# Fused thresholded attention and hard-swish layer: another order of work in the last slots and the tail

## The chip, the cores and the metric

One core of a Trainium2 chip runs the whole kernel. The metric is the time of one execution on the device, in microseconds (us); for the kernel before it is 521.78 us, the median of three runs (521.37 to 523.26). Profiles are of one execution; their span (521.3 us for the kernel before) is counted from its first to its last instruction. TensorE multiplies, VectorE and ScalarE work on the results, GpSimd does one step of the softmax, and SyncE's queue issues most transfers.

## The reference

Attention over 8 batches, 8 heads, 576 tokens and 64 dimensions, in which scores that lie more than `tau` below the row's maximum are rejected, and then a layer with two products and a hard-swish between them over all 4608 tokens:

```
scores = (q @ k.T) / sqrt(64)
scores = where(scores >= max(scores) - tau, scores, -1e9)
attn   = exp(scores - max(scores));  attn = attn / (sum(attn) + 1e-9)
x      = (attn @ v), heads side by side           # 4608 x 512
h      = x @ w_in                                 # 4608 x 2048
g      = h * clip(h + 3, 0, 6) / 6
out    = g @ w_out                                # 4608 x 512, f32
```

## The kernel before

**Slots.** The 64 heads are taken in 16 groups of four (a "quad", two pairs of heads). A batch has two quads. The 576 query rows are four blocks of 128 and a remainder of 64. Each quad has nine slots: four blocks for each pair, and one slot for the remainder rows of both pairs. So there are 144 slots, numbered 0 to 143, and one loop that runs over them (L518). In slot n the scores of slots further on are multiplied (`scores`, L287, one or two slots ahead), VectorE takes the maximum of slot n + 1 while it copies the scores out of PSUM (`sm_max`, L302), ScalarE masks and exponentiates (L309, L314), VectorE takes the reciprocal of the sums (L317), GpSimd multiplies by it (`sm_norm`, L322), and a DMA transpose issued by SyncE (L330) turns the rows of attention around for the product with the values (`av`, L346 and L349). The transposed tiles are called `pT` for the blocks of 128 rows and `pR` for the remainder slot.

**The layer.** It follows behind the attention, item by item. An *item* (`mm1`) is a first product of 512 columns in one PSUM bank: eight products 256 wide for the main tokens (L381), or four products 512 wide for the *odd tokens*, the 64 remainder rows of two batches together (L376). ScalarE (L389) or VectorE (L391) forms the clamp `r` from it, and VectorE gates it (`mm1_gate`, L404) into `g`. The clamp has two tiles. For odd tokens the gate writes a separate tile `go`, two items to a tile, and a DMA transpose (L406) brings that into `g`; there is one `go` tile only, so the third odd gate can't begin before the first transpose has read it. A *token tile* (`mm2_part`, four parts of four products) is 128 tokens of the second product: 16 products 512 wide (L415), an eviction with the factor 1/6 (L421 on ScalarE, L423 on VectorE) and a store (L436).

**Queues.** `todo1` holds items, `todo2` holds parts of token tiles; a tile's parts enter `todo2` when the last item that it needs has been multiplied. Each slot takes one item, each even slot two parts as well. `moe_of(b)` lists the items of batch b: the columns 0 to 255 first, in eight items, then the odd tokens (batches with odd numbers only, four items), then the columns 256 to 511 in eight items. For odd batches the last two odd items are put behind two of the others (L447).

**Banks.** PSUM has eight banks (`ps`). In the loop, items and tile parts use the banks 6 and 7 (`HB`, `OB`), scores 0, 1, 3, 4 and halves of 2 and 5, and the attention product 2 and 5. An even slot's item and the following odd slot's share bank 6 if the even slot had tile parts.

**The tail.** All of this is written out by hand: each engine does its work in the order in which the program lists it. After the loop there is (L649 to L663): the third quarter of the last quad's attention product, the two items left in `todo1` (batch 6, clamp on VectorE), the reciprocal and the multiplication for slot 143, the eight *head* items of batch 7, the last attention product of the blocks and that of the remainder rows (`av_rest`), all tile parts that wait in `todo2`, the twelve *tail* items of batch 7 (four odd items, eight main ones) and the last three token tiles. Here the items go round the banks 0, 1, 3 and 4 (`rest1`, beginning with bank 1), and the tiles alternate between the banks 7 and 6 (`rest2`).

Of the kernel before, what the change touches and what calls it, by code (L numbers as in the profile page):

```python
# [20 lines left out]
def kernel(  # L21
# [11 lines left out]
    B, H, S, D = q.shape  # L33
# [8 lines left out]
    N1 = 22  # L42
    N2 = 28
    HB, OB = 6, 7
# [138 lines left out]
    def warm_up(count):  # L183
        for _ in range(count):
            nc.tensor.transpose(ps[:, HB, 0:P], identf[:], identf[:])
# [23 lines left out]
    now = -1  # L209
    turn = 0  # L210

    def bank():
        nonlocal turn
        turn += 1
        return ps[:, (2, 5)[turn % 2], :]
# [96 lines left out]
    def sm_exp(sl, i):  # L312
        s = sl.s[:, i, :]
        nc.scalar.activation(out=s, in_=s, func=Act.Exp, accum_out=sl.rsum[:, i:i + 1])  # L314

    def sm_recip(sl):
        nc.vector.reciprocal(out=sl.rinv[:], in_=sl.rsum[:])  # L317
# [23 lines left out]
    def av(pb, pair, pT, cols):  # L341
        b, hp = divmod(pair, NPAIR)
        vm, vr = vsb[b]
        for c in range(4):
            for a in range(2):
                nc.tensor.matmul(pb[a * 64:(a + 1) * 64, :], vm[:, 2 * hp + a, c * D:(c + 1) * D],  # L346
                                 pT[:, 5 * a + c, cols], start=(c == 0), stop=False)
        for a in range(2):
            nc.tensor.matmul(pb[a * 64:(a + 1) * 64, :], vr[:, a, hp, :], pT[:, 4, cols], start=False, stop=True)  # L349

    def av_main(pair, c0=0, w=512):
        b, hp = divmod(pair, NPAIR)
        if hp == c0 == 0:
            xT[b] = x_pool.tile([P, KI, 512], BF16, tag="xT", name="xT")
        pb = bank()[:, 0:w]
        av(pb, pair, pts[pair], slice(c0, c0 + w))
        return lambda: nc.vector.tensor_copy(out=xT[b][:, hp, c0:c0 + w], in_=pb)  # L357
# [14 lines left out]
    def mm1(item, hb=HB):  # L372
        b, ni, c0 = item
        if c0 is None:
            for ki in range(KI):
                nc.tensor.matmul(ps[:, hb, :], xR[b // 2][:, ki, :], w_in_sb[:, ki, ni * P:ni * P + 512],  # L376
                                 start=(ki == 0), stop=(ki == KI - 1))
        else:
            for n in range(2):
                for ki in range(KI):  # L380
                    nc.tensor.matmul(ps[:, hb, n * 256:(n + 1) * 256], w_in_sb[:, ki, (ni + n) * P:(ni + n + 1) * P],  # L381
                                     xT[b][:, ki, c0:c0 + 256], start=(ki == 0), stop=(ki == KI - 1))
        return ps[:, hb, :]
# [27 lines left out]
    def mm2_part(bb, mt, part, ob=OB):  # L411
        if part == 0:
            o_ps[0] = ps[:, ob, :]
        for ni in range(part * 4, part * 4 + 4):
            nc.tensor.matmul(o_ps[0], gbuf[:, ni, mt * P:(mt + 1) * P], w_out_sb[:, ni, :],  # L415
                             start=(ni == 0), stop=(ni == NI - 1))
# [14 lines left out]
    todo2 = []  # L431
# [8 lines left out]
    def moe_of(b):  # L440
        items = []
        for c0, mts in (((0, (5, 6)), (None, (4,)), (256, (7, 8))) if b % 2 else ((0, (0, 1)), (256, (2, 3)))):
            for ni in range(0, NI, 4 if c0 is None else 2):
                items.append(((b, ni, c0), ()))
            items[-1] = (items[-1][0], [(b // 2, mt, part) for mt in mts for part in range(4)])
        if b % 2:
            items[10:14] = items[12:14] + items[10:12]  # L447
        return items[0:8], items[8:]

    alloc_qk(0)  # L450
# [18 lines left out]
    queue = []  # L469
# [34 lines left out]
    def multiply(n):  # L504
# [6 lines left out]
                todo1.extend(moe_of(of // 2)[0])  # L511
        return copies

    prev = None
    last_keys = []
    part = 0
    waiting = []
    for n, sl in enumerate(queue):  # L518
        quad, slot = sl.quad, sl.slot
        b, g = divmod(quad, 2)  # L520
        now = n
        if slot in (0, 4):
            pts[2 * quad + slot // 4] = pt_pool.tile([P, 9, 512], BF16, tag="pT", name="pT")
        if slot == 8:
            ptr[quad] = ptr_pool.tile([P, 9, P], BF16, tag="pR", name="pR")
        for ahead in {0: (1, 2), 9: (3,), 16: (4,)}.get(n, (quad + 2,) if quad > 2 and slot == (2 if quad == 3 else 0) else ()):
            if ahead < NQUAD:
                load_quad(ahead)
        if slot == 0 and g == 1 and b + 1 < B:
            load_v(b + 1)  # L530
        for copy in last_keys:
            copy()
        last_keys = []
        if 0 < n <= N1:
            for i in range(2):
                sm_exp(prev, i)
        if n + 1 < len(queue):
            sm_max(queue[n + 1])
        even = n >= N1 and n % 2 == 0
        if n > N1:  # L540
            sm_recip(prev)
        for copy in waiting:
            copy()
        waiting = []

        if todo1:
            item, then = todo1.pop(0)
            h = mm1(item, OB if n > N1 and n % 2 and not pieces else HB)
            todo2.extend(then)
        else:  # L550
            item = None
        if n >= N1:
            for copy in multiply(n):
                copy()
        if item:
            mm1_gate(item, h, mm1_relu(h, on_act=even))
        copies = pe_transpose(queue[n - 2]) if n > 1 and queue[n - 2].on_chip else None
        if prev is not None and n < N1:
            sm_recip(prev)
        if copies:  # L560
            copies()
        pieces = 2 if n % 2 == 0 and todo2 else 0
        for _ in range(pieces):
            bb, mt, part = todo2.pop(0)
            mm2_part(bb, mt, part)
        if n <= N1:
            for i in range(2):
                sm_mask(sl, i)
        if n == N1:
            sm_recip(prev)  # L570
        if n >= N1:
            for i in range(2):
                sm_exp(sl, i)
            if n + 1 < len(queue):
                for i in range(2):
                    sm_mask(queue[n + 1], i)
        if n < N1:
            for copy in multiply(n):
                copy()
        if part == 3:  # L580
            waiting.append(lambda tile=(bb, mt): late.extend(mm2_out(*tile, on_act=False)))
            part = 0
        evict = []
        for job, of in turns.get(n, ()):
            if job == "k":
                (last_keys if even else evict).append(transpose_k(of))
            elif job == "q":
                if of // 2 not in qkT:
                    alloc_qk(of // 2)
                (waiting if even else evict).append(transpose_q(of))  # L590
            else:
                (last_keys if even else evict).append(transpose_rest(of, of_k=of > 0))
        for out_of_psum in evict:
            if out_of_psum:
                out_of_psum()
        if n == 0:
            warm_up(8)
        if n <= N1:
            scores(n + 2)
        elif n % 2:  # L600
            for m in (n + 3, n + 2):
                if m < len(queue):
                    scores(m)
        if n < 8:
            warm_up(6)
        if n > 0:
            sm_norm(prev)
        flush()
        if n == 0:
            start(loads, 2)  # L610
        elif n not in (4, 12, 15, 18, 21) and not 23 < n < 30 and (n < 37 or n % 2 == 0):
            start(loads, 1)
        if n < 4 or 15 < n < 20 or n > 33:
            start(vcasts, 1 if n < N1 or n % 2 else 0)
        else:
            start(casts, 2 if n in (5, 8, 11, 14) or 21 < n < 28 else 1)
        prev = sl
# [13 lines left out]
    def rest1(item, then, on_act=True):  # L631
        h = mm1(item, hb=(0, 1, 3, 4)[count[0] % 4])
        count[0] += 1
        mm1_gate(item, h, mm1_relu(h, on_act))
        todo2.extend(then)

    def rest2():
        while todo2:
            bb, mt, part = todo2.pop(0)
            mm2_part(bb, mt, part, ob=OB - count[1] % 2)  # L640
            if part == 3:
                flush()
                if (bb, mt) == (B // 2 - 1, 8):
                    last_out()
                else:
                    late.extend(mm2_out(bb, mt, on_act=(count[1] % 2 == 0)))
                count[1] += 1
# [4 lines left out]
    sm_recip(prev)  # L652
    sm_norm(prev)
    head, tail = moe_of(B - 1)
    for item in head:
        rest1(*item)
    av_main(2 * last + 1, 256, 256)()
    av_rest(last)()
    rest2()
# [38 lines left out]
```

## Time and profile before

| what | value |
|---|---|
| time, median of three runs | 521.78 us (521.37 to 523.26) |
| span of the profiled execution | 521.3 us |
| TensorE busy | 503.0 us, 96% of the span |
| VectorE, ScalarE busy | 442.5 us (85%), 451.9 us (87%) |
| GpSimd busy | 299.3 us (57%) |
| slot 142's item begins on TensorE | 464.49 us |
| the tail's first items begin (L381 x80) | 469.27 us |
| `av_rest` begins | 479.77 us |
| tile parts between head and tail begin (L415 x70) | 480.44 us |
| tail items begin (L376) | 495.76 us |
| last three token tiles begin, TensorE ends | 507.16 us, 517.5 us |

In a timeline, a line has the start, the length, the engine, the line of the kernel, the operation with its output and input tiles and shapes, and a count of instructions that were merged; in brackets stand the idle time of the engine ahead of it and what ended it. PE is TensorE's stream of products, PEld its loading of weights, DVE is VectorE, ACT ScalarE, POOL GpSimd and SPq the queue of SyncE. The ends of products are modelled, and a few per cent of their records can be missing (70 of 72 products have one in a group above).

### The profile page before, as it was taken

What the parts mean: (1) busy time and instruction counts of PE and PEld (TensorE: products, weight loads), DVE (VectorE), ACT (ScalarE), POOL (GpSimd) and SP (SyncE); (2) the same over time, 40 slices, a digit from 0 to 9 for tenths busy, and PEclk for the clock granted to TensorE, in tenths of its full rate; (3) what the DMA queues carried; (4) which work ended last, traced back from release to release, by engine and by line L of the source; (5) the groups of instructions that cost most, each with busy time, mean ns of one, the idle gap of its engine ahead of it and who ended that gap; (6) DMA issues with size and microseconds to landing.
All of it is one profiled execution on the core that took longest, in us unless ns stands there. A gap on an engine that the chain in (4) does not pass through costs nothing.

```text
span 521.3 us, 12068 instructions
## 1 busy us (share of the span) xinstructions
PE 503.0 (96%) x4089; PEld 321.4 (62%) x4145; DVE 442.5 (85%) x1124; ACT 451.9 (87%) x980; POOL 299.3 (57%) x538
## 2 busy tenths in 40 slices
PE   8999999999999999999999999999999999999997
PEld 6765556666665666666665666666655666667463
DVE  3788888998999989999999999999999999877151
ACT  3999979999999989999999999999999999995060
POOL 1788869756676656657566656657566755551000
PEclk9999999999999999999999999999999999999999
DMA  5899999999999999999989999999999996574222
GB/s 131 123 174 157 155 150 139 152 177 177 160 168 178 160 181 168 173 165 187 178 148 162 181 179 160 176 159 177 165 160 171 183 162 113 112 117 65 82 61 60
DMA packets 314094, 78.77 MB, mean 151 GB/s; under 512 B 296624, under 2 KB 309168, under 8 KB 314032
## 3 DMA queue, kind: packets, MB, share of 16 engines
q1 hardware_dynamic: 294464, 67.90, 77.6%
q0 software_dynamic: 18368, 9.71, 15.7%
q8 instruction: 32, 0.52, 0.4%
q10 hardware_dynamic: 1200, 0.39, 0.3%
q14 instruction: 30, 0.25, 0.2%
HBM read 36.70 MB, written 9.44 MB: 89 GB/s over the span
## 4 chain that ended last, share of the span: by engine, by line
PE 69%; ACT 5%; DMA 4%; DVE 3%; issue 2%; POOL 2%; SPq 1%; POOLq 0%; DVEq 0%
PE ps L287 22%; PE ps L415 21%; PE ps L381 18%; PE ps L346 6%; PE ps L376 2%; ACT s L309 2%; DMA pT<-pn 2%; POOL pn L322 2%; ACT s L314 2%; DVE s L302 1%; ACT r L389 1%; PE ps L349 1%; DMA pR<-pn 1%; DVE g L404 1%; DMA nq<-in_q_dram 1%
## 5 line engine op out<-in xcount | busy, mean ns | idle before, releaser
L322 POOL TENSOR_SCALAR pn<-s,rinv 128x576 bf16<-128x576 f32 x288 | 210.6, 743 | 19.1 <-issue 4.4
L302 DVE TENSOR_SCALAR_CACHE_REDUCE s<-ps 128x576 f32<-128x576 f32 x288 | 205.1, 749 | 17.6 <-PE ps L287 9.0
L309 ACT ACTIVATE s<-s,bias 128x576 f32<-128x576 f32 x288 | 205.8, 763 | 6.0 <-POOL bias L305 5.7
L314 ACT ACTIVATE s<-s 128x576 f32<-128x576 f32 x288 | 192.5, 671 | 0.3
L287 PE MATMUL ps<-kT,qT 64*128 64x384 f32 (+7 forms) x1280 | 174.0, 419 | 4.7 <-DVE s L302 3.8
L287 PEld LDWEIGHTS ps<-kT,qT 64*128 64x128 f32 (+1 forms) x1280 | 103.6, 175 | 59.3 <-issue 15.8
L381 PE MATMUL ps<-xT,w_in_sb 128*128 128x256 bf16 x1024 | 130.8, 273 | 1.2 <-DVE g L404 0.7
L415 PE MATMUL ps<-w_out_sb,g 128*128 128x512 bf16 x524 | 123.4, 379 | 2.8 <-issue 0.2
L381 PEld LDWEIGHTS <-w_in_sb 128*128 128x128 bf16 x1024 | 95.5, 98 | 41.0 <-issue 22.0
L305 POOL TENSOR_SCALAR bias<-m 128x2 f32<-128x2 f32 x144 | 26.9, 187 | 155.5 <-DVE rinv L317 135.8
L404 DVE SCALAR_TENSOR_TENSOR g<-r,ps 128x512 bf16<-128x512 f32 x128 | 87.6, 687 | 9.5 <-ACT r L389 5.5
L415 PEld LDWEIGHTS <-g 128*128 128x128 bf16 x576 | 56.3, 98 | 56.6
L389 ACT ACTIVATE r<-ps,three 128x512 f32<-128x512 f32 x81 | 55.4, 687 | 29.9 <-PE ps L381 20.9
L314 ACT ACTIVATION_READ_ACCUMULATOR s<-s 128x1 f32 x288 | 54.6, 189 | 0.0
L391 DVE TENSOR_SCALAR r<-ps 128x512 f32<-128x512 f32 x63 | 42.9, 681 | 0.0
L346 PE MATMUL ps<-pT,vm 128*64 128x256 bf16 (+1 forms) x480 | 39.1, 285 | 0.9 <-DMA pT<-pn 0.9
L346 PEld LDWEIGHTS <-vm 128*64 128x64 bf16 x736 | 27.4, 110 | 17.9 <-issue 16.3
L357 DVE CAST xT<-ps 128x256 bf16<-128x256 f32 (+1 forms) x60 | 26.3, 438 | 13.8 <-PE ps L349 13.8
L423 DVE TENSOR_SCALAR osb<-ps 128x512 f32<-128x512 f32 x31 | 20.9, 673 | 13.3 <-PE ps L415 13.3
L302 DVE DVE_READ_ACCUMULATOR s<-ps 128x1 f32 x288 | 23.9, 83 | 0.0
L317 DVE RECIPROCAL rinv<-rsum 128x2 f32<-128x2 f32 x144 | 23.0, 160 | 0.6 <-ACT s L314 0.6
L143 POOL DMA_DIRECT2D vm<-in_v_dram x28 | 21.4, 766 | 0.7 <-issue 0.7
(57 smaller groups left out, 259.4 us busy)
## 6 DMA issues: line engine op xcount, KB each, us to landing
out_dram<-osb SPq DMA_DIRECT2D x31, 256.0 KB, 2.7
nq<-in_q_dram SPq DMA_DIRECT2D x96, 72.0 KB, 3.5
km<-in_k_dram SPq DMA_DIRECT2D x96, 64.0 KB, 3.2
vm<-in_v_dram POOLq DMA_DIRECT2D x24, 128.0 KB, 4.2
km<-in_k_dram SPq DMA_DIRECT2D x16, 128.0 KB, 3.5
w_in_sb<-in_moe_w_in_dram POOLq DMA_DIRECT2D x16, 128.0 KB, 3.8
w_out_sb<-in_moe_w_out_dram POOLq DMA_DIRECT2D x16, 128.0 KB, 6.2
pT<-pn SPq DMA_TRANSPOSE x117, 4.1
```

The source lines that it names most:

```text
L287: nc.tensor.matmul(ps_flat[rows, c0:c0 + w], qT_of(pair)[a * 64:(a + 1) * 64, q0:q0 + rows.stop - rows.start], kT_of(pair)[a * 64:(a + 1) ...
L302: nc.vector.tensor_scalar(out=sl.s[:, i, :], in0=ps_flat[:, c0:c0 + S], scalar1=1.0, scalar2=None, op0=Alu.mult, op1=Alu.max, accum_out=sl ...
L305: nc.gpsimd.tensor_scalar(out=sl.bias[:], in0=sl.m[:], scalar1=-scale, scalar2=tau, op0=Alu.mult, op1=Alu.add)
L309: nc.scalar.activation(out=s, in_=s, func=Act.Prelu, bias=sl.bias[:, i:i + 1], scale=scale, alpha=REJECT)
L314: nc.scalar.activation(out=s, in_=s, func=Act.Exp, accum_out=sl.rsum[:, i:i + 1])
L322: nc.gpsimd.tensor_scalar(out=pn[:, i, :], in0=sl.s[:, i, :], scalar1=sl.rinv[:, i:i + 1], scalar2=1.0, op0=Alu.mult, op1=Alu.mult)
L346: nc.tensor.matmul(pb[a * 64:(a + 1) * 64, :], vm[:, 2 * hp + a, c * D:(c + 1) * D], pT[:, 5 * a + c, cols], start=(c == 0), stop=False)
L381: nc.tensor.matmul(ps[:, hb, n * 256:(n + 1) * 256], w_in_sb[:, ki, (ni + n) * P:(ni + n + 1) * P], xT[b][:, ki, c0:c0 + 256], start=(ki = ...
L389: nc.scalar.activation(out=r, in_=hps, func=Act.Relu, bias=three[:])
L391: nc.vector.tensor_scalar(out=r, in0=hps, scalar1=3.0, scalar2=0.0, op0=Alu.add, op1=Alu.max)
L404: nc.vector.scalar_tensor_tensor(out=out, in0=r, scalar=6.0, in1=hps, op0=Alu.min, op1=Alu.mult)
L415: nc.tensor.matmul(o_ps[0], gbuf[:, ni, mt * P:(mt + 1) * P], w_out_sb[:, ni, :], start=(ni == 0), stop=(ni == NI - 1))
```

## The change

Three edits, none of which adds or removes any arithmetic:

- In slot 142 the two parts of a token tile go ahead of the slot's item. Slot 143's item is put into bank 0, since it now follows slot 142's directly and would share bank 6 with it. For this, the code that takes parts from `todo2` becomes a function, `second`.
- After the loop, the tile parts that are left over are multiplied ahead of the last head item and of the last attention products, and no longer behind them. It is meant to give the transfer of the remainder rows work to lie beside.
- In the last batch, four main items lie between the second and the third odd item where there were two, so that the first and third odd item are six apart. It is meant to give the transpose of the first two odd items time to give back `go`.

```diff
@@ -443,8 +443,10 @@ def moe_of(b):
-        if b % 2:
+        if b % 2 and b < B - 1:
             items[10:14] = items[12:14] + items[10:12]
+        elif b % 2:
+            items[10:16] = items[12:16] + items[10:12]
         return items[0:8], items[8:]
@@ -511,9 +513,16 @@
+    def second():
+        nonlocal pieces, bb, mt, part
+        pieces = 2 if now % 2 == 0 and todo2 else 0
+        for _ in range(pieces):
+            bb, mt, part = todo2.pop(0)
+            mm2_part(bb, mt, part)
+
     prev = None
     last_keys = []
-    part = 0
+    pieces = bb = mt = part = 0
@@ -545,7 +554,9 @@
         if todo1:
             item, then = todo1.pop(0)
-            h = mm1(item, OB if n > N1 and n % 2 and not pieces else HB)
+            if n == len(queue) - 2:
+                second()
+            h = mm1(item, 0 if n == len(queue) - 1 else OB if n > N1 and n % 2 and not pieces else HB)
             todo2.extend(then)
@@ -559,10 +570,8 @@
-        pieces = 2 if n % 2 == 0 and todo2 else 0
-        for _ in range(pieces):
-            bb, mt, part = todo2.pop(0)
-            mm2_part(bb, mt, part)
+        if n != len(queue) - 2:
+            second()
@@ -652,8 +661,10 @@
     head, tail = moe_of(B - 1)
-    for item in head:
+    for item in head[0:7]:
         rest1(*item)
+    rest2()
+    rest1(*head[7])
     av_main(2 * last + 1, 256, 256)()
     av_rest(last)()
     rest2()
```

## The prediction

> **What bounds the kernel now.** I read the page's first part, then the order of time on TensorE over the last 60 us, then what VectorE, ScalarE and the queue of SyncE do beside it.
>
> ```profile
> span 521.3 us, 12068 instructions
> ...
> PE 503.0 (96%) x4089; PEld 321.4 (62%) x4145; DVE 442.5 (85%) x1124; ACT 451.9 (87%) x980; POOL 299.3 (57%) x538
> ```
>
> TensorE is the bound, and in the part that the diff touches (from slot 142 on) it is almost alone: from 480 us on VectorE and ScalarE mostly wait for it. Its time can then only fall by closing gaps. These are TensorE's lines around the gaps, from the timeline (start, length, line, what; in brackets the idle time ahead and its releaser):
>
> ```profile
> 462.58 1.25 PE L287 MATMUL ps<-kT,qT 64*64 64x320 f32 x16
> 464.49 1.03 PE L381 MATMUL ps<-xT,w_in_sb 128*128 128x256 bf16 x8 [0.66 <-DVE g L404]
> 465.58 1.67 PE L415 MATMUL ps<-w_out_sb,g 128*128 128x512 bf16 x7
> ...
> 469.27 8.91 PE L381 MATMUL ps<-xT,w_in_sb 128*128 128x256 bf16 x80
> 478.11 0.63 PE L346 MATMUL ps<-pT,vm 128*64 128x256 bf16 x8
> ...
> 479.77 0.32 PE L346 MATMUL ps<-pR,vm 128*64 128x64 bf16 x8 [0.93 <-DMA pR<-pn]
> ...
> 480.44 15.49 PE L415 MATMUL ps<-w_out_sb,g 128*128 128x512 bf16 x70 [0.16 <-issue]
> ...
> 503.45 3.65 PE L381 MATMUL ps<-xT,w_in_sb 128*128 128x256 bf16 x32 [0.58 <-DVE go L404]
> 507.16 10.31 PE L415 MATMUL ps<-w_out_sb,g 128*128 128x512 bf16 x47
> ```
>
> Three waits and one small gap: 0.66, 0.93, 0.58 and 0.16 us, in all 2.33 us. That is the ceiling, give or take the modelled ends (the projection that follows a full pair of score groups begins at 451.63, 0.07 us before the modelled end of those, 449.49 + 2.21), so I allow 0.07 more for each of the three waits: 2.5 us.
>
> Two lines of other engines carry the rest of the argument, VectorE's around the first gap and its wait behind the third:
>
> ```profile
> 467.61 0.17 DVE L317 RECIPROCAL rinv<-rsum 128x2 f32<-128x2 f32 x1 [0.64 <-ACT s L314]
> 468.83 0.42 DVE L357 CAST xT<-ps 128x256 bf16<-128x256 f32 x1 [1.06 <-PE ps L349]
> ...
> 472.87 0.69 DVE L404 SCALAR_TENSOR_TENSOR g<-r,ps 128x512 bf16<-128x512 f32 x1
> ```
>
> ```profile
> 502.71 1.29 DVE L404 SCALAR_TENSOR_TENSOR go<-r,ps 128x512 bf16<-128x512 f32 x2 [1.87 <-DMA g<-go]
> ```
>
> See in the first that from 468.83 on VectorE runs without a break to beyond 473.5; in the second that the third gate of odd tokens waits for the first transpose to give back the only `go` tile.
>
> **What the Trainium skill says.** "TensorE: Matmul & The Clock Gate", section "Back-to-back issue gap", gives about 216 ns for a product 512 wide. The trace agrees: 72 products from 480.44 to 495.76 are 213 ns each, so a moved tile (16 products, 3.4 us) costs the same wherever it stands. Its section "Architectural detail: the array is 16× 32×32, not 1× 128×128" says that ScalarE and VectorE are strictly first in, first out. The trace agrees: the gate of odd tokens that waits at 502.71 holds up VectorE's next gates, and through the clamp tiles that these would free, ScalarE's next clamp, which waits 1.65 us. "DMA: Bandwidth & Descriptors", section "Rules for kernel authors", says to issue a transfer early and wait for it late; the 0.93 us wait is a breach of it (issued at 475.27, wanted at about 478.8, there at 479.73).
>
> **Part 1: slot 142.** Before: the projection of slot 142 goes into bank 6, whose last user, slot 141's gate, ends at about 464.45, so TensorE waits 0.66 us; then come eight second products. After: those eight go first, from 463.83; their operand and bank 7 have been ready since the eviction of 461.86 (0.67 us long). The eight take 1.7 us, the projection follows at 465.55 and slot 143's right behind it. That one would have waited for slot 142's gate in bank 6; bank 0 spares it that, since its last reader, the maximum of slot 142, was done by 461.9. TensorE reaches the first leftover item 0.66 us sooner, at 468.6 for 469.27. The rows of attention that it needs on the way were issued at 463.73 and took 3.6 us (the landing of that transpose): there at 467.3, wanted at about 468.0.
> The added wait: ScalarE's clamp of slot 142 starts 465.55 - 464.49 = 1.06 us later, and behind it stand two exponentials, two masks and two more exponentials; VectorE's reciprocal at 467.61 moves to 468.67. VectorE had 1.06 us of idle time after it, so its next copy starts at about 468.8, as before. VectorE thus gains nothing, and its chain runs unbroken to the gate at 472.87. Count the banks: the explicit tail cycles through 1, 3, 4, 0, so the sixth item after the loop (fourth of the head) takes the bank of the second. It would start 5 x 0.884 us (10 items from 469.27 to 478.11) after the first: 473.69 before, 473.03 after. But the second item's gate frees the bank only at about 473.5. TensorE therefore waits some 0.45 us there, and of the 0.66 us **0.2 us** stays. The bounds are 0 (VectorE a little late as well) and 0.66.
>
> **Part 2: leftover tiles ahead of the last products.** When the head begins, 40 second products are left over (half a tile and two tiles, all of batch 6 and so ready). Before, they stood behind the two attention products of the last pair. After, they stand between the seventh and eighth head items: 40 x 0.213 = 8.5 us. The transpose of the remainder rows lands at 479.73 as before, and is wanted only at about 477 + 8.5 + 0.9 + 0.7 = 487. The whole **0.93 us** goes. What was queued behind the wait (remainder rows, their copy, the tiles of batch 7, the tail) comes forward by it. New waits: the eighth head item feeds the first tile of batch 7, but only at its 15th product, 0.7 + 0.35 us of attention and 14 x 0.213 = 3.0 us after that item; its clamp and gate take 0.69 + 0.69 us, hidden. The two banks alternate as before and each eviction (0.6 to 0.7 us) lies beside a tile of 3.4 us. The 0.16 us gap after the short products comes with them and stays. One more change between kinds of product (0.05 us of "issue" in the chain of waits) I count as -0.05.
>
> **Part 3: odd items six apart.** Time from the tail's start (495.76 before). Before: the second odd gate ends at 3.4, the transpose is issued at 3.43 (499.19), and lands in 3.1 us; VectorE can write `go` again at 6.95 (502.71). The third odd gate, two even items after the second, was due at about 5.3 and waits 1.87 us; ScalarE has only two clamp tiles and stops; TensorE, four banks ahead, loses 0.58. After: four even items lie between. At 0.87 us an item the third odd gate is due at 1.84 + 6 x 0.87 = 7.05, just after 6.95. So the **0.58 us** goes; were it 0.1 to 0.3 late, four banks would hide it.
> The price is on the other side: the second transpose is issued two items later than need be. The fourth odd gate ends at about 8.5, the transpose lands 3.1 us later (both of this tail took 3.1) at 11.65, perhaps 12.1 if the waiter wakes as late as VectorE did (0.44 us after landing). The first token tile to need it starts at 10.66 (11.40 before, less the gap as start to start, 503.45 - 502.71) and wants it after eight products, at 12.35. No wait, but with only 0.25 to 0.7 us to spare; before, some 2 us were. The other eight gates of the tail end by 12 and are wanted later.
>
> **Sum.** 0.2 + 0.93 - 0.05 + 0.58 = 1.66 us; nothing after TensorE's last product changes (two half evictions and a store, 3.8 us). 521.78 - 1.66 = **520.1 us**.
>
> **Rivals.**
> - *All gaps close* (14%): VectorE in slots 142 and 143 moves forward with TensorE, so that 0.66 stays, and the modelled ends add 0.07 each: 0.66 + 0.93 + 0.58 + 0.2 = 2.4, 519.4 us. For it: the items are paced by TensorE before. Against it: the unbroken VectorE chain from 468.83 on.
> - *ScalarE's delay gets through* (12%): the 1.06 us are not absorbed ahead of the copy at 468.83, so the gate chain of the head shifts by them. The gain of 0.2 becomes a loss of 0.86, and the sum 0.6: 521.2 us. For it: slack and delay are equal to the last digit. Against it: the delay would have to miss the slack entirely.
> - *The second transpose comes late* (8%), the slower side: transposes of this kind took up to 6.0 us from issue to landing elsewhere in the kernel. Then it lands at 8.55 + 6.0 = 14.55, 2.2 us after it is wanted, and the sum turns into -0.55: 522.3 us. For it: the thin margin. Against it: both in this tail took 3.1, with nothing but one store beside them, as now.
> - The forecast, 520.1 us: 66%.
>
> **How the numbers follow.** The forecast and the first two rivals (92%) lie between 519.4 and 521.2; the three runs of before lie 0.4 below to 1.5 above their median, so I take 519.2 to 521.6. Faster by over 0.5% would mean below 519.17, past the ceiling of 2.5 us or nearly: half of the first rival and a little scatter, 9%. Slower by over 0.5%, above 524.39, only an unseen cause can give: 3%. The rest, 88%, within 0.5%.
>
> **What the profile after would show.** Part 1: second products start at about 463.8 without a gap, ScalarE's clamp of slot 142 about 1 us later, and a new wait of some 0.45 us on a gate within the head's items (none: first rival; over 1 us: second). Part 2: the wait on the transpose of the remainder rows is gone and nothing waits between the head and the tail. Part 3: the wait of VectorE for the first `go` transpose falls from 1.87 us to under 0.3, TensorE's 0.58 is gone, and a wait on the second transpose ahead of the last tiles is absent or below 0.2. The forecast is wrong if a new wait appears in the 40 products, or if the work before slot 142 differs.

## The result, and the profile after

520.06 us, median of four runs (519.97 to 520.21), against 521.9 us for the kernel before, with a fourth run (521.37 to 523.26): a ratio of 0.9961, interval 0.9942 to 0.998. So the change makes the kernel 1.84 us faster (the interval is 1.0 to 3.0 us), where 1.66 us to 520.1 us had been forecast.

The first part of the page:

```profile
span 518.3 us, 12124 instructions
...
PE 505.9 (98%) x4145; PEld 321.1 (62%) x4145; DVE 442.6 (85%) x1124; ACT 452.1 (87%) x980; POOL 299.3 (58%) x538
```

The span is 3.0 us shorter, more than the times say. The difference arose ahead of the change: slot 143's scores, which no edit touches, begin at 461.62 us here and at 462.58 us before. In the loop between 150 and 460 us TensorE at times waits for a transpose of attention rows, and that differs from run to run, though no edit touches that part: the kernel before waits 0.9 us there, once, the changed kernel not at all, and an experiment below 2.4 us. For this reason I count from slot 143's scores on.

TensorE's timeline of the changed kernel, the lines that answer to those shown of before:

```profile
461.62 1.25 PE L287 MATMUL ps<-kT,qT 64*64 64x320 f32 x16
462.80 1.90 PE L415 MATMUL ps<-w_out_sb,g 128*128 128x512 bf16 x8
464.54 1.91 PE L381 MATMUL ps<-xT,w_in_sb 128*128 128x256 bf16 x16
...
467.59 4.71 PE L381 MATMUL ps<-xT,w_in_sb 128*128 128x256 bf16 x40
472.49 3.65 PE L381 MATMUL ps<-xT,w_in_sb 128*128 128x256 bf16 x32 [0.19 <-DVE g L404]
475.98 8.80 PE L415 MATMUL ps<-w_out_sb,g 128*128 128x512 bf16 x40
484.62 1.04 PE L381 MATMUL ps<-xT,w_in_sb 128*128 128x256 bf16 x8
...
486.04 0.28 PE L349 MATMUL ps<-pT,vr 128*64 128x256 bf16 x2
486.15 0.29 PE L346 MATMUL ps<-pR,vm 128*64 128x64 bf16 x8
...
486.44 0.20 PE L349 MATMUL ps<-pR,vr 128*64 128x64 bf16 x2
486.57 7.08 PE L415 MATMUL ps<-w_out_sb,g 128*128 128x512 bf16 x32
493.48 1.89 PE L376 MATMUL ps<-w_in_sb,xR 128*128 128x512 bf16 x8
495.21 3.66 PE L381 MATMUL ps<-xT,w_in_sb 128*128 128x256 bf16 x32
498.70 1.89 PE L376 MATMUL ps<-w_in_sb,xR 128*128 128x512 bf16 x8
500.43 3.66 PE L381 MATMUL ps<-xT,w_in_sb 128*128 128x256 bf16 x32
503.92 10.52 PE L415 MATMUL ps<-w_out_sb,g 128*128 128x512 bf16 x48
```

The three waits of before have no counterpart. One new wait stands in brackets, ahead of the sixth item after the loop: there the forecast had put it. The bracket says 0.19 us, but the wait costs more. The Trainium skill, "TensorE: Matmul & The Clock Gate", section "Step-by-step: what each phase is for", says that the drain of one product overlaps the start of the next. The trace agrees: a 256-wide product lasts 0.27 us, and they start 0.109 us apart (32 from 500.43 to 503.92). So a gap has to be measured from start to start. Five items should take 40 x 0.109 = 4.4 us; from 467.59 to 472.49 they take 4.9, so the wait costs 0.5 us.

By landmarks, then: A is the start of slot 143's scores, B that of the first leftover item, C that of the first tail item, D the start of ScalarE's half eviction of the last token tile (TensorE's end). Each row is one profiled execution. All in us:

| kernel | A | A to B | B to C | C to D | A to D | less than before |
|---|---|---|---|---|---|---|
| before | 462.58 | 6.69 | 26.49 | 21.74 | 54.92 | |
| changed | 461.62 | 5.97 | 25.89 | 21.00 | 52.86 | 2.06 |
| part 1 alone | 464.14 | 5.98 | 26.89 | 21.75 | 54.62 | 0.30 |
| part 2 alone | 463.18 | 6.69 | 25.37 | 21.34 | 53.40 | 1.52 |
| part 3 alone | 463.12 | 6.69 | 26.63 | 21.00 | 54.32 | 0.60 |
| item 143 in bank 6 | 462.42 | 7.63 | 25.37 | 21.00 | 54.00 | 0.92 |
| five apart | 461.69 | 5.98 | 25.89 | 21.00 | 52.87 | 2.05 |
| eight apart | 461.58 | 5.97 | 25.89 | 22.28 | 54.14 | 0.78 |
| tiles ahead of the head | 463.73 | 5.97 | 25.37 | 21.00 | 52.34 | 2.58 |
| clamp 142 on VectorE | 462.18 | 5.98 | 25.37 | 21.00 | 52.35 | 2.57 |

Where TensorE waits for no transfer, directly or through VectorE, the same code takes the same time to 0.02 us from kernel to kernel (5.97 or 5.98, 25.37, 25.89, 21.00), far closer than whole runs do. Where it does wait for one, that isn't so: from B to C the kernel before and part 3 alone have the same order of work and take 26.49 and 26.63 us, and from C to D the kernel before and part 2 alone take 21.74 and 21.34 us. The verdicts below rest on this table. Whole runs agree with it, but loosely: the last column lies inside the interval of each kernel's ratio.

### The profile page after: what moved, and what is told of

The parts are those of the page before. It is cut to its first block, busy times and chain, and to the rows that moved or that the text cites. A ratio compares the mean times of both kernels' runs of the same rounds, so it can differ in the third digit from the quotient of the medians.

```text
span 518.3 us, 12124 instructions
## 1 busy us (share of the span) xinstructions
PE 505.9 (98%) x4145; PEld 321.1 (62%) x4145; DVE 442.6 (85%) x1124; ACT 452.1 (87%) x980; POOL 299.3 (58%) x538
## 4 chain that ended last, share of the span: by engine, by line
PE 81%; ACT 3%; DVE 2%; POOL 0%; issue 0%; POOLq 0%
PE ps L287 25%; PE ps L415 24%; PE ps L381 21%; PE ps L346 7%; PE ps L376 3%; ACT s L314 1%; PE ps L349 1%; ACT s L309 1%; DVE g L404 1%; ACT r L389 1%; DVE s L302 0%; DVE r L391 0%; POOL pn L322 0%; PE ps L257 0%; ACT kT L222 0%; DVE xT L357 0%
## 5 line engine op out<-in xcount | busy, mean ns | idle before, releaser
L415 PE MATMUL ps<-w_out_sb,g 128*128 128x512 bf16 x576 | 134.1, 379 | 0.0
```

## The experiments

Each edit is given against the kernel before or against the changed one. The times are medians; the kernel before had 522.54 us beside the first four and 522.45 us beside the last four.

**Part 1 alone** (the kernel before with `second` and bank 0).

```diff
+            if n == len(queue) - 2:
+                second()
-            h = mm1(item, OB if n > N1 and n % 2 and not pieces else HB)
+            h = mm1(item, 0 if n == len(queue) - 1 else OB if n > N1 and n % 2 and not pieces else HB)
...
-        pieces = 2 if n % 2 == 0 and todo2 else 0
...
+        if n != len(queue) - 2:
+            second()
```

> Part 1 alone (slot 142's tile parts ahead of its item, slot 143's item in bank 0). Theory: from slot 143's scores to the first leftover item 5.97 us as in the changed kernel (6.69 before), then TensorE waits about 0.45 us in the head's fourth item, and what stays is mostly taken by the wait for the remainder rows' transpose, which grows by about 0.15 us because that transpose hangs on VectorE's chain and not on TensorE. Total gain 0.15 us, 521.6 to 521.8. Rival (the parts simply add): 0.3 us. Rival (ScalarE's delay gets through): a loss of 0.5 us or more.

Measured: 522.65 us, ratio 1.0001 (0.9988 to 1.0014); by landmarks 0.30 us less. TensorE's lines, around the two waits that are left:

```profile
470.12 4.71 PE L381 MATMUL ps<-xT,w_in_sb 128*128 128x256 bf16 x40
475.02 4.53 PE L381 MATMUL ps<-xT,w_in_sb 128*128 128x256 bf16 x40 [0.19 <-DVE g L404]
...
481.03 0.32 PE L346 MATMUL ps<-pR,vm 128*64 128x64 bf16 x8 [0.82 <-DMA pR<-pn]
```

The item's wait appears at the sixth item as in the changed kernel: A to B falls by 0.71 us and B to C grows by 0.40. The wait for the remainder rows didn't grow, against the theory. TensorE waits for their transpose to land, so the gain is what the landing gained: the transpose is issued 12.54 us after A for 12.69 in the kernel before, 0.15 us sooner, and took 4.30 us for 4.46, 0.16 less. Only the first follows from the order of work as far as the runs show; over all kernels this transpose took 3.9 to 5.1 us. So the 0.15 us of the theory and the rival's 0.3 can't be told apart here. The second rival, a loss of 0.5 us or more, didn't come.

**Part 2 alone** (the kernel before; `second` is there too, but is called where the loop took the parts before).

```diff
-    for item in head:
+    for item in head[0:7]:
         rest1(*item)
+    rest2()
+    rest1(*head[7])
```

> Part 2 alone (left-over tiles ahead of the last head item). Theory: from the first leftover item to the first tail item 25.5 us (26.5 before), the wait of 0.93 us for the remainder rows gone, nothing in its place; total gain 1.0 us, 520.9. Rival (a new wait among the moved tiles or behind the eighth head item takes its place): gain below 0.5 us.

Measured: 521.56 us, ratio 0.9973 (0.9953 to 0.9994). B to C falls by 1.12 us, with no wait in it. C to D falls by 0.40 us too, which was not expected. 0.06 us of it is an earlier landing of the first transpose of odd tokens (6.45 us after C for 6.51). The rest is that in the kernel before and in part 1 alone the third odd gate began about 0.44 us after that landing; here 0.10 us. The chain of waits of the kernel before:

```profile
499.19 3.08 DMA g<-go
502.27 0.03 issue
502.29 0.02 DVEq L404
502.31 0.40 issue
502.71 0.70 DVE go L404
```

and of part 2 alone:

```profile
498.60 3.09 DMA g<-go
501.69 0.03 issue
501.72 0.02 DVEq L404
501.74 0.04 issue
501.79 0.70 DVE go L404
```

The transfers are equal (3.08 and 3.09 us); VectorE's sequencer sees each at once (the `DVEq` lines), and then one gate starts 0.40 us later, the other 0.04 us. Why, the runs don't show, nor whether part 2 is the cause or only this execution.

**Part 3 alone.**

```diff
-        if b % 2:
+        if b % 2 and b < B - 1:
             items[10:14] = items[12:14] + items[10:12]
+        elif b % 2:
+            items[10:16] = items[12:16] + items[10:12]
```

> Part 3 alone (odd items six apart). Theory: from the first tail item to TensorE's end 21.0 us (21.7 before), VectorE's wait of 1.87 us for the first transpose of odd tokens gone, no wait on the second; total gain 0.74 us, 521.1. Rival (second transpose late): TensorE waits 1 to 2 us ahead of the last tiles, a loss.

Measured: 522.26 us, ratio 0.9994 (0.9981 to 1.0008). C to D is 21.00 us, 0.74 less, as expected. B to C, which the edit doesn't touch, is 0.14 us longer: the transpose of the remainder rows took 4.6 us. The three parts alone add to 2.42 us, together they bring 2.06. The main reason is that 0.40 us of part 3's 0.74 are the same as those that part 2's run saved from C to D, and can't be saved twice. The rest is the remainder rows' transpose: 0.10 us more in part 1 alone than in the whole change, 0.14 less here.

**Slot 143's item in bank 6** (in the changed kernel).

```diff
-            h = mm1(item, 0 if n == len(queue) - 1 else OB if n > N1 and n % 2 and not pieces else HB)
+            h = mm1(item, OB if n > N1 and n % 2 and not pieces else HB)
```

> The changed kernel, but slot 143's item stays in bank 6. Theory: it waits for slot 142's gate, some 1.6 us, and the first leftover item comes 1.6 us later (7.5 us after slot 143's scores for 5.97); the wait of some 0.45 us in the fourth head item then vanishes, since TensorE is no longer ahead of VectorE; total 1.1 us above the changed kernel, 521.1 to 521.2. Rival (the bank is of no matter, the attention products between hide it): as the changed kernel, 520.0.

Measured: 521.36 us, ratio 0.998 (0.9969 to 0.999). TensorE's timeline:

```profile
465.33 1.04 PE L381 MATMUL ps<-xT,w_in_sb 128*128 128x256 bf16 x8
467.87 1.03 PE L381 MATMUL ps<-xT,w_in_sb 128*128 128x256 bf16 x8 [1.50 <-DVE g L404]
...
470.05 8.03 PE L381 MATMUL ps<-xT,w_in_sb 128*128 128x256 bf16 x72
```

A to B grows by 1.66 us, and the wait among the head's items is gone (72 products in one line), as theory had it: B to C 25.37. The loss against the changed kernel is 1.14 us. Without bank 0 the new order of slot 142 would have cost 0.94 us from A to B, not gained 0.72.

**Five apart and eight apart** (in the changed kernel: three and six main items between the second and the third odd item).

```diff
-            items[10:16] = items[12:16] + items[10:12]
+            items[10:15] = items[12:15] + items[10:12]
```

> The changed kernel with three main items, not four, between the second and third odd item (first and third five apart). Theory: the third odd gate waits 0.3 to 0.7 us for the first transpose, TensorE's lead of four banks hides it, and from the first tail item to TensorE's end it stays 21.0 us; the second transpose lands 0.87 us sooner. Total as the changed kernel. Rival (every wait of VectorE here is TensorE's loss): 21.3 to 21.7 us.

Measured: 520.07 us, ratio 0.9957 (0.9942 to 0.9971); C to D 21.00. VectorE's wait for the first transpose is back:

```profile
DVE go L404 <- DMA g<-go: 0.9, 1, 0.9
```

and TensorE doesn't wait: its four banks cover 0.9 us, though not the 1.87 us of the kernel before. Three items would have done. The expected 0.87 us for the second transpose came to 0.40, since the third odd gate waits: it is issued 8.19 us after C (501.75 less 493.56) for 8.59 in the changed kernel (502.07 less 493.48).

```diff
-            items[10:16] = items[12:16] + items[10:12]
+            items[10:18] = items[12:18] + items[10:12]
```

> The changed kernel with six main items between the second and third odd item (eight apart). Theory: the second transpose is issued about 10.4 us after the first tail item and lands at 13.5; the last tiles want it at 12.15 us, so TensorE waits about 1.3 us there: 22.3 us from the first tail item to TensorE's end for 21.0. Total 1.3 us above the changed kernel. Rival (the margin is wider than computed, as the tile has other parts to do): as the changed kernel.

Measured: 521.81 us, ratio 0.9988 (0.998 to 0.9995); C to D 22.28, as computed. TensorE's timeline:

```profile
503.88 1.89 PE L415 MATMUL ps<-w_out_sb,g 128*128 128x512 bf16 x8
506.88 8.81 PE L415 MATMUL ps<-w_out_sb,g 128*128 128x512 bf16 x39 [1.10 <-DMA g<-go]
```

After the first eight products of the last tiles it waits for the second transpose. The margin that six apart leaves is thus as narrow as computed: the issue moves by two items of 0.87 us, 1.74, and TensorE loses 1.28, so 0.46 us were to spare.

**The left-over tiles ahead of the whole head** (in the changed kernel).

```diff
-    for item in head[0:7]:
+    rest2()
+    for item in head:
         rest1(*item)
-    rest2()
-    rest1(*head[7])
```

> The changed kernel with the left-over tiles ahead of the whole head, not only of its last item. Theory: VectorE catches up beside the 8.5 us of tile products, so the wait in the head's fourth item (0.4 to 0.5 us) is gone; from the first leftover item to the first tail item 25.4 us for 25.9, all else the same; 0.45 us below the changed kernel. Rival (the wait only moves, to the head's last items or to the remainder rows' transpose): 25.9 us or more.

Measured: 520.24 us, ratio 0.9955 (0.9936 to 0.9974); B to C 25.37, 0.52 less than the changed kernel, no wait from A to D. The median of the whole runs doesn't show it (520.06 for the changed kernel), the fastest run does (519.55 for 519.97); A lies 2.1 us later in the profiled run, the slowest of the six, where TensorE waits 1.4 us for transposes in the loop.

**Slot 142's clamp on VectorE** (in the changed kernel).

```diff
-            mm1_gate(item, h, mm1_relu(h, on_act=even))
+            mm1_gate(item, h, mm1_relu(h, on_act=even and n != len(queue) - 2))
```

> The changed kernel with slot 142's clamp on VectorE, so that ScalarE's exponentials of that slot don't wait for the late item. Theory (ScalarE's delay is what holds VectorE's chain back in the changed kernel): VectorE's reciprocal of slot 142 no longer waits for ScalarE, its copy for slot 143 starts about 0.5 us sooner after slot 143's scores (5.6 us for 6.1), and the wait in the head's fourth item all but vanishes: from the first leftover item to the first tail item 25.4 to 25.5 us for 25.9. Rival (VectorE is slow there by its own work, of which this adds 0.68 us): 26.0 us or more.

Measured: 519.78 us, ratio 0.9948 (0.9933 to 0.9963), the lowest median of all; B to C 25.37. VectorE's lines of the changed kernel:

```profile
466.33 0.69 DVE L404 SCALAR_TENSOR_TENSOR g<-r,ps 128x512 bf16<-128x512 f32 x1 [1.43 <-ACT r L389]
467.66 0.17 DVE L317 RECIPROCAL rinv<-rsum 128x2 f32<-128x2 f32 x1 [0.64 <-ACT s L314]
467.74 0.40 DVE L357 CAST xT<-ps 128x256 bf16<-128x256 f32 x1
```

and of this one:

```profile
466.18 0.69 DVE L391 TENSOR_SCALAR r<-ps 128x512 f32<-128x512 f32 x1 [0.71 <-PE ps L381]
467.51 0.16 DVE L317 RECIPROCAL rinv<-rsum 128x2 f32<-128x2 f32 x1
467.72 0.43 DVE L357 CAST xT<-ps 128x256 bf16<-128x256 f32 x1
```

In the first the reciprocal ends a wait for ScalarE and the copy follows it at once, 6.12 us after A. In the second the reciprocal waits for nothing, and the copy starts 5.54 us after A, although VectorE does one operation of 0.69 us more: it now starts 0.04 us behind the modelled end of TensorE's product (467.68), as in the kernel before (468.79). So in the changed kernel ScalarE's delay is what holds VectorE's chain, and with it TensorE at the sixth item.

## Why the prediction was right, step by step

**Part 1, 0.2 us forecast, 0.20 measured** (beside the other two parts). TensorE is 0.72 us sooner at B (forecast 0.66) and loses 0.52 us (0.45) at the sixth item, the one that had been named, on the gate of the second. The mechanism was right; that the size is right to the last digit is luck, since two terms were too small by 0.06 and 0.07 us and cancel. The step "ScalarE's clamp starts 1.06 us later, VectorE's copy stays where it was" held nearly: the clamp starts 3.99 us after A for 2.98 before, 1.01 us later, and the copy 6.12 for 6.25. The first rival, in which all gaps close, didn't come true in the changed kernel. Two experiments reach what it would have given, by removing the cause: 2.58 and 2.57 us. The three gaps from start to start are 0.72, 1.12 and 0.74 us, 2.58 in all, so the ceiling of 2.5 us that the forecast named was a little low. The second rival's mechanism was there, ScalarE's delay, but the slack took it up as forecast.

**Part 2, 0.93 - 0.05 us forecast, 1.12 measured.** The mechanism was right, the term too small. The bracket of 0.93 us leaves out the part of the gap that lies beside a modelled end. The last product ahead of the wait in the kernel before is this one:

```profile
478.57 0.28 PE L349 MATMUL ps<-pT,vr 128*64 128x256 bf16 x2
```

From it to 479.77 it is 1.20 us from start to start, for 0.11 in the changed kernel (486.04 to 486.15), so the wait had cost 1.09. The 0.05 us for one more change of products didn't appear. Nothing took the wait's place.

**Part 3, 0.58 us forecast, 0.74 measured.** Again the size alone: the 16 products ahead of the gap begin at 500.96 and follow at 0.109 us each, so the next was due at 502.71 and came at 503.45, 0.74 us late. The forecast had worked this number out for the margin and yet put 0.58 into the sum. Of the 0.74 us, 0.40 were already gone in the run of part 2 alone, so what part 3 adds to it is 0.34. The third odd gate starts 7.01 us after C, for a forecast of 7.05, and waits for no transfer. The third rival, the late second transpose, is the true limit of the edit, but lies 0.46 us away; eight apart shows it.

**The sum** was 0.4 us too small by landmarks (2.06 for 1.66), and nearer to the medians' 1.84, which can't tell the two apart: their interval is 1.0 to 3.0 us. That the median came out at 520.06 us for a forecast of 520.1 is thus in part luck. The small gap of 0.16 us, counted to the ceiling, isn't one. Where all records are there (x32 at 486.57) products follow at 0.13 us. In these timelines "0.16 <-issue" stands only where records are missing (70 of 72, 31 of 32, seven of eight): it is a missing first record.

The same record makes the forecast's pace of 213 ns for a product 512 wide a little short. Without it only 71 products, not 72, lie between 480.44 and 495.76, at 216 ns each; 40 from 475.98 to 484.62 in the changed kernel, all recorded, give 216 ns too. The section of the Trainium skill that the forecast cites, "Back-to-back issue gap", states its 216 ns for an isolated product and 131 ns for products that each have their weights loaded. Here each has (72 loads to the 72 products), and the measured 216 ns decides. Nothing in the sum hangs on this.

## What to carry to other kernels

Price a gap from the start of the last product ahead of it to the start of the next one, less the usual distance: brackets left out 0.06 to 0.33 us of each here. When one engine's wait is closed, look for whose buffer it runs into next and by how much: 0.72 us became 0.20 because a bank came free on another engine's old schedule. And where a transfer's wait is moved rather than removed, compute the margin at the far end too; three items between gave the same time with the second transpose 0.40 us earlier.

## What was not expected of the hardware

- A VectorE instruction that waits for a transfer began about 0.44 us after the landing in three kernels (the one before, part 1 alone, five apart) and 0.10 us after it in a fourth (part 2 alone). In the chains shown above its sequencer was awake after 0.02 to 0.03 us either way. The cause is open.
- The last transpose of remainder rows took 3.9 to 5.1 us from issue to landing over the ten kernels, each of the two transposes of odd tokens in the tail 3.1 us in all of them. Run to run, TensorE waits from nothing to 2.4 us for transposes in the loop: as much as the whole change is worth.
